# The second layer's second product, in its last two passes, by a seven-product scheme over two quads at a time

## The chip, the cores and the metric

One NeuronCore of a Trainium2 chip runs the whole program. The metric is the device time of one execution in microseconds; less is better. The engines that matter here are PE (TensorE: matrix products, with PEld for its weight loads), DVE (VectorE), ACT (ScalarE), and SP (SyncE), whose queue issues every transfer. POOL (GpSimd) works in the first quarter only.

## The reference

```python
def _moe_ref(x, w_in, w_out):            # first layer, after the attention
    h = x @ w_in
    relu6 = np.clip(h + 3.0, 0.0, 6.0)
    g = h * relu6 / 6.0
    return (g @ w_out).astype(np.float32)

def _moe2_ref(x, w_in, w_out):           # second layer
    h = x @ w_in
    g = np.maximum(0.01 * h, h)
    return (g @ w_out).astype(np.float32)

def reference(...):
    attn_out = _attn_ref(q, k, v)        # 4 x 8 heads, 576 tokens, window 64
    x = attn_out laid out as 2304 tokens x 512
    return _moe2_ref(_moe_ref(x, moe_w_in, moe_w_out), moe2_w_in, moe2_w_out)
```

There are 2304 tokens, the model width is 512 and the hidden width 2048. Inputs and outputs are fp32.

## The kernel before, in words

Every large product is made in pieces of a 128x128 stationary tile and a moving tile of 256 to 512 columns. Each operand is kept as a high half (`h`) and a low half (`l`), both fp32r, and a product is three matmuls: high by high, low by high, high by low. Making the two halves of a tile is a copy (ACT, `copy`, L322) and a subtraction (DVE, `tensor_tensor`, L332).

The first 240 us hold the attention and the first six hidden blocks of the first layer. From there on the hidden width goes in *quads*: 256 hidden columns by 768 tokens by 512 inputs, cut into 2x2x2 blocks. The first product of a quad (x by `w_in`) takes seven block products in place of eight (`SEQ`, the scheme of Strassen in Winograd's form; the matmul is L889, six of 384 columns in each block product, 42 in a quad). The blocks of weights for it are made once (`convert_quad`), written to DRAM (`kept`) and read back in each pass (`fetch`).

The second layer has three passes over the tokens (`NPAIR`, 768 tokens each), and in each pass eight quads. In the first pass the weights of quads 4 to 7 are still being converted; those of quads 0 to 3 were converted ahead, during the first layer. After the seven block products DVE adds partial sums (`plus`, L337), ACT applies the leaky rectifier (L865, L870), and the four blocks C11, C12, C21, C22 are split into halves. The second product (g by `w_out`, `outputs1`, the matmul is L1012) is plain: four blocks by three chunks of 128 tokens by three matmuls, 36 of 512 columns in a quad. It adds up in six PSUM banks over all eight quads, and is copied out once a pass. The outputs of quad i run between the block products of quad i+1, at places that `FILL` names: six units of three matmuls after M6 and six after M7.

The second product of the first layer (`outputs0`, L960) has pieces of 512 and of 256 columns.

The order of the work is written out by `Order`: each step is recorded with what it reads and writes and with an estimated cost; the steps are then placed on the engines, and each engine runs its list in that order. The products of PE are chained, so their order is the one in which they are recorded. On each engine an instruction waits for its inputs and for the buffers it overwrites, and what stands behind it waits too.

## Time and profile before

| | |
|---|---|
| time, median of 3 runs | 849.51 us (847.99 to 850.63) |
| the profiled execution | 850.17 us, of which its span 848.1 us |
| PE busy | 830.9 us, 98% of the span |
| PEld busy | 739.3 us, 87% |
| DVE busy | 540.5 us, 64% |
| ACT busy | 505.9 us, 60% |
| DMA | 201.26 MB, mean 237 GB/s |

The span runs from the first to the last instruction. A row of the timeline gives start, duration, engine, line, operation and the tiles written and read. Matmuls are pipelined: the duration of one is longer than the distance between two starts, so the rate is read from starts. The tiles `h` and `a` and `y` are PSUM banks; `w0h` and `w0l` hold blocks of `w_in`, `w1h` and `w1l` those of `w_out`.

### The profile page before, as it was taken

The page shows a single profiled execution, that of the slowest core. Times are in us where ns is not written, and L with a number is a line of the kernel's source. Part 1 is how long each engine was busy: PE and PEld are TensorE (multiplying, and loading weights), DVE is VectorE, ACT ScalarE, POOL GpSimd, SP SyncE. Part 2 cuts the span into 40 slices and gives each one's busy share as a digit, 9 for nine tenths or more (in the row PEclk, how much of TensorE's full clock was granted, in tenths as well). Part 3 has the DMA queues.
Part 4 walks back from the last instruction along what each step waited for, and adds up shares of the span by engine and source line. Part 5 has one row for each costly group of instructions (what it writes and reads, how often), then busy time and mean ns, then how long its engine had stood idle before and what let it go on. Part 6 is the DMA issues. An engine that isn't in the chain of part 4 may idle for free.

```text
span 848.1 us, 14685 instructions
## 1 busy us (share of the span) xinstructions
PE 830.9 (98%) x5254; PEld 739.3 (87%) x5254; DVE 540.5 (64%) x1184; ACT 505.9 (60%) x1146; POOL 42.5 (5%) x45
## 2 busy tenths in 40 slices
PE   7799999999999999999999999999999999999998
PEld 5578888888999999999999999898998899899986
DVE  5999777878868788878879848888222235222221
ACT  4988878776766665566568457676433344432333
POOL 2222221210000000000000000000000000000000
PEclk9999999999999999999999999999999999999999
DMA  8957485638775879998898747679755564765501
GB/s 272 338 173 262 124 288 200 234 128 281 249 289 186 300 283 319 339 374 270 291 385 304 266 157 251 234 241 366 258 199 166 186 208 158 265 213 163 174 24 75
DMA packets 106329, 201.26 MB, mean 237 GB/s; under 512 B 10768, under 2 KB 22544, under 8 KB 106256
## 3 DMA queue, kind: packets, MB, share of 16 engines
q1 hardware_dynamic: 106256, 200.32, 69.0%
q8 instruction: 42, 0.69, 0.4%
q14 instruction: 31, 0.25, 0.1%
HBM read 153.35 MB, written 46.92 MB: 236 GB/s over the span
## 4 chain that ended last, share of the span: by engine, by line
PE 94%; DVE 2%; DMA 2%; ACT 1%; SPq 0%; issue 0%; DVEq 0%
PE h L889 33%; PE y L1012 16%; PE y L960 9%; PE y L652 9%; PE h L606 9%; PE a L1012 8%; PE a L960 5%; PE a L496 2%; PE h L553 1%; PE a L521 1%; DMA qt<-in_q_dram 1%; DMA st<-in_moe_w_out_dram 1%; PE y L496 1%; DVE ca L360 0%; SPq L340 0%
## 5 line engine op out<-in xcount | busy, mean ns | idle before, releaser
L337 DVE TENSOR_TENSOR qt<-h,qt 128x384 f32<-128x384 f32 x69 | 38.5, 557 | 112.4 <-PE h L889 61.8
L889 PE MATMUL h<-e,w0h 128*128 128x384 f32 x354 | 105.7, 335 | 0.0
L889 PE MATMUL h<-e,w0l 128*128 128x384 f32 x348 | 104.6, 336 | 0.1
L1012 PE MATMUL y<-w1h,at 128*128 128x512 f32 x288 | 97.2, 391 | 0.0
L322 ACT ACTIVATE qt<-h 128x384 f32<-128x384 f32 x77 | 37.6, 488 | 72.0 <-PE h L889 71.8
L960 PE MATMUL y<-at,w1h 128*128 128x512 f32 x240 | 79.4, 391 | 0.0
L889 PE MATMUL h<-xa,w0h 128*128 128x384 f32 x236 | 69.5, 335 | 0.0
L889 PE MATMUL h<-xa,w0l 128*128 128x384 f32 x232 | 68.6, 335 | 0.0
L889 PEld LDWEIGHTS h<-e,w0h 128*128 128x128 f32 x354 | 65.5, 188 | 0.9
L889 PEld LDWEIGHTS h<-e,w0l 128*128 128x128 f32 x348 | 64.4, 188 | 1.3 <-ACT qt L322 0.5
L1012 PEld LDWEIGHTS y<-w1h,at 128*128 128x128 f32 x288 | 54.1, 188 | 10.5
L360 DVE TENSOR_SCALAR ca<-ca 128x512 f32<-128x512 f32 (+1 forms) x128 | 56.3, 447 | 5.5 <-ACT ca L371 4.3
L1012 PE MATMUL y<-w1l,at 128*128 128x512 f32 x144 | 56.6, 393 | 0.0
L960 PEld LDWEIGHTS y<-at,w1h 128*128 128x128 f32 x240 | 45.1, 188 | 8.8
L337 DVE TENSOR_TENSOR r<-h,r 128x384 f32<-128x384 f32 x32 | 17.8, 557 | 53.0 <-ACT r L322 30.2
L1012 PE MATMUL a<-w1h,at 128*128 128x512 f32 x144 | 50.2, 389 | 0.0
L333 POOL TENSOR_TENSOR at<-at,rc 128x512 f32<-128x512 f32 (+1 forms) x36 | 41.1, 1144 | 138.7 <-DVE rc L452 80.3
L960 PE MATMUL a<-at,w1h 128*128 128x256 f32 x240 | 47.8, 282 | 0.0
L960 PE MATMUL y<-at,w1l 128*128 128x512 f32 x120 | 47.2, 394 | 0.0
L371 ACT ACTIVATE ca<-st 128x512 f32<-128x512 f32 x64 | 42.7, 669 | 6.5 <-DMA st<-in_moe_w_out_dram 3.0
L652 PE MATMUL y<-gh,w1h 128*128 128x512 f32 (+1 forms) x120 | 45.8, 382 | 0.0
L332 DVE CUSTOM_DVE_ANT_0 ca<-ca,cr 128x1024 uint16<-128x1024 uint16 x64 | 44.7, 703 | 0.6
(261 smaller groups left out, 2086.0 us busy)
## 6 DMA issues: line engine op xcount, KB each, us to landing
w0h<-kept SPq DMA_DIRECT2D x116, 256.0 KB, 4.1
w0l<-kept SPq DMA_DIRECT2D x115, 256.0 KB, 4.2
w1h<-kept SPq DMA_DIRECT2D x66, 256.0 KB, 4.5
w1l<-kept SPq DMA_DIRECT2D x66, 256.0 KB, 4.8
st<-in_moe_w_in_dram SPq DMA_DIRECT2D x32, 512.0 KB, 5.1
st<-in_moe_w_out_dram SPq DMA_DIRECT2D x32, 512.0 KB, 5.1
kept<-e SPq DMA_DIRECT2D x33, 256.0 KB, 3.7
kept<-gh SPq DMA_DIRECT2D x22, 256.0 KB, 5.4
```

The lines of the kernel that those rows point to most:

```text
L322: a = act(n, lambda: nc.scalar.activation(out=dst(), in_=src(), func=AF.Copy, scale=scale))
L332: d = dve(n, lambda: nc.vector.tensor_tensor(out=dst(), in0=a(), in1=b(), op=alu))
L333: p = pool(n, lambda: nc.gpsimd.tensor_tensor(out=dst(), in0=a(), in1=b(), op=alu))
L337: return [dve(n, lambda: nc.vector.tensor_tensor(out=dst(), in0=a(), in1=b(), op=alu))]
L360: return dve(DM, lambda: nc.vector.tensor_scalar(out=dst(), in0=src(), scalar1=s1, scalar2=s2, op0=op0, **({"op1": op1} if op1 else {})), ...
L371: act(DM, lambda: nc.scalar.activation(out=af(), in_=high().bitcast(F32), func=AF.Abs)),
L496: nc.tensor.matmul(pp()[part * W:(part + 1) * W, c * L:(c + 1) * L], y()[r, i, c, :], x()[r, c, j * W:j * W + L], start=not early, stop=Tr ...
L606: nc.tensor.matmul(ph()[:, 0:n], wt()[:, cs], xt()[:, 0:n], start=(c == 0 and m == 0), stop=(c == NK - 1 and m == 2),)
L652: nc.tensor.matmul(y()[:, 0:n], stat()[:, cs], mov()[:, 0:n], start=(first and m == 0), stop=(last and m == 2))
L889: nc.tensor.matmul(bk()[:, 0:HT], a, b_(), start=(start and j == 0 and q_ == 0), stop=(j == 1 and q_ == 2), skip_group_check=True,)
L960: nc.tensor.matmul(y()[:, d:d + n], a()[:, cs], b_[1]()[:, t0:t0 + n], start=(begins and m == 0), stop=(last and m1 and m == 2), skip_grou ...
L1012: nc.tensor.matmul(y(), a()[:, cs], b_(), start=(first and m == 0), stop=(last and m == 2))
```

## The change

In passes two and three of the second layer the second product also takes seven block products in place of eight, over two quads at a time (`outputs2`). Its blocks are two token halves by two hidden blocks by two halves of the output width, and the two quads of a pair are added up inside PSUM. One block product is three chunks of 128 tokens by two quads by three matmuls, each of 256 columns: 18, and 126 for a pair of quads. Its left operands are A11, A12, A22 and four combinations S1 to S4 (made by DVE in `quad`, and split into halves like the others), its right operands six blocks of `w_out` and of differences of its blocks, made in `convert_quad` (four more tiles for a quad, written to `kept`). They are read back by column halves, in runs of 1 KB (`fetch_y`), into a ring of eight tiles.

PSUM no longer holds the outputs of a pass. Two pairs of banks (`up`, `side`) take the block products in turn, and after each one DVE adds the bank into a sum in SBUF (`add`: one piece of 512 columns and one of 256; in the first pair of a pass some are copies on ACT). There are seven such additions in a pair. The banks `a` now serve the first product of every second quad. `YPLAN` puts the block products of the outputs between those of the first product, one at a time.

Beside that, `xb` (the second layer's input) is three tiles in place of one, so that its parts can be used again as room for the A and S blocks; the ring of `w1` tiles has 6 in place of 7, and the staging ring `st` 4 in place of 3.

```diff
+    WRING = {"w0h": RING, "w0l": RING, "w1h": RING - 1, "w1l": RING - 1}
+    ST = 4
...
-    xb = const.tile([P, NK, NT], F32, name="xb")
...
-    kept = [[dr.tile([11 * P, DM], F32, name=f"kept{j}_{i}") for i in range(n)] for j, n in enumerate(QUADS)]
+    kept = [[dr.tile([(15 if j else 11) * P, DM], F32, name=f"kept{j}_{i}") for i in range(n)] for j, n in enumerate(QUADS)]
...
+    XT = 2 * HT
+    xbt = [buf(f"xb{r}", [P, NK * XT], F32, 1) for r in range(NPAIR)]
...
+    YPLAN = ((0, 1, 0, 1, 1, 0, 1), (0, 1, 0, 1, 1, 0, 0))
...
+            got = [od.slot(("stage", layer), None, None, None, 0, stage_homes(layer)) for _ in range(15 if layer else 11)]
...
+            if layer:
+                got += [od.slot("spare", None, None, None, 0, spare_homes()) for _ in range(4)]
...
+            outs.append((a, af))
+        if layer:
+            (b1, b1f), (b2, b2f) = outs
+
+            def minus(t, tf, h, x, y, reads):
+                op(tensor_tensor(256, lambda: tf()[:, h], x, y, ALU.subtract), reads, [t])
+
+            minus(b1, b1f, L, lambda: b1f()[:, R], lambda: b1f()[:, L], [b1])
+            minus(b1, b1f, R, lambda: b2f()[:, R], lambda: b1f()[:, R], [b1, b2])
+            halves(DM, b1f, [b1], got[11], got[12], got[11], got[12])
+            minus(b2, b2f, R, lambda: b2f()[:, R], lambda: b1f()[:, L], [b1, b2])
+            minus(b2, b2f, L, lambda: b2f()[:, L], lambda: b2f()[:, R], [b2])
+            halves(DM, b2f, [b2], got[13], got[14], got[13], got[14])
+            for j in range(11, 15):
+                keep(j)
...
+    def spare_homes():
+
+        if "spare" not in stage:
+            gone = after_reads(range(1))
+            stage["spare"] = [
+                (None, gone, lambda c=c: xb(c, 0, DM).bitcast(F32R)) for c in range(NK)
+            ]
+        return stage["spare"]
...
+            up, side = bank(tag, 2), bank(tag, 2)
+            twice = "S1" in slots
...
-                    value(r12, *slots["C12"])
+                    if twice:
+                        op(steep(r12), [r12], [r12])
+
+                        def part(t, name):
+                            (kh, h_), (kl, l_) = slots[name]
+                            halves(HT, t, [t], kh, kl, h_, l_)
+
+                        def mix(t, x_, y_, alu):
+                            op(tensor_tensor(HT, t, x_, y_, alu), [x_, y_], [t])
+
+                        mix(r22, r12, r22, ALU.add)
+                        part(r22, "S1")
+                        mix(r12, r11, r12, ALU.subtract)
+                        mix(r11, r22, r11, ALU.subtract)
+                        part(r11, "S2")
+                        part(r12, "S3")
+                        mix(r21, r21, r11, ALU.subtract)
+                        part(r21, "S4")
...
-                            if p < NPAIR - 1:
-                                t = buf("st", [P, DM, 2], U32, bufs=3)
-
-                                def z():
...
-                            else:
-                                t = z = buf(f"xs{c}{'hl'[half]}", [P, DM], F32, 1)
...
+                            k = 3 * half + c
+                            t = sums[k]
+
+                            def z():
+                                return t()[:, 0:DM].bitcast(F32)
+
+                            op(copy(DM, z, y), [y], sum_keys(k))
+                            load_out(P * DM * 4, out[r0:r0 + P, :], z, sum_keys(k))
...
+        YSEQ = (("M1", "A11"), ("M2", "A12"), ("M6", "S2"), ("M5", "S1"), ("M7", "S3"), ("M3", "S4"), ("M4", "A22"))
+        YROWS = {"M1": (7, 0), "M2": (9, 0), "M3": (9, 1), "M5": (11, 0), "M7": (11, 1), "M4": (13, 0), "M6": (13, 1)}
...
+        def settle(early):
+
+            sums.extend(buf(t, [P, DM], F32R, WRING[t]) for t in ("w1h", "w1l") * 3)
+            ywt.extend((None, t, t) for t in [buf(t, [P, DM], F32R, WRING[t]) for t in ("w1h", "w1l") * 3])
+            xbt[0].ops += [*early.prev[1].ops, *(i for t in od.tags[("ring", "spare")] for i in t.ops)]
+            xbt[1].ops += after_reads(range(1, 3)).prev[1].ops
+            free = [buf(f"xb{r}", [P, NK * XT], F32R, 1) for r in range(2)]
...
+            order = units[0:8] + units[16:26] + units[8:16] + old
...
+        def outputs2(p, n, pairs):
+
+            first, last = n == 0, n == QUADS[1] // 2 - 1
+            up = bank("y0"), bank("y1")
+            side = bank("y2"), bank("y3")
+            tiles_ = {}
+
+            def fetch_y(m):
+                hi, half = YROWS[m]
+                for e in range(2):
+                    t = tiles_[m, e] = od.slot("yw", None, None, None, 0, ywt)
+                    src = kept[1][2 * n + e][hi * P:(hi + 2) * P, half * 256:half * 256 + 256].rearrange(
+                        "(m p) n -> p m n", p=P)
+                    load(P * DM * 4, lambda t=t: t().bitcast(F32).rearrange("p (m n) -> p m n", m=2), src, [t],
+                         [("kept", 1, 2 * n + e, hi + j) for j in range(2)])
+
+            def add(b, bk, fresh):
+                i, j = b // 2, b % 2
+                for w, k, o, y in ((DM, b, 0, bk[0]), (256, 4 + i, 256 * j, bk[1])):
+                    t = sums[k]
+                    keys = sum_keys(k) if w == DM else [(t, j)]
+
+                    def dst(t=t, o=o, w=w):
+                        return t()[:, o:o + w].bitcast(F32)
+
+                    def got(y=y, w=w):
+                        return y()[:, 0:w]
+
+                    if fresh:
+                        op(copy(w, dst, got), [y], keys)
+                    else:
+                        op(vector_only(w, dst, got, dst, ALU.add), [y, *keys], keys)
+
+            def send(b):
+                i, j = b // 2, b % 2
...
+            def product(m, x, bk, start):
+                wt = [tiles_[m, e] for e in range(2)]
+                gs_ = [pairs[e][x] for e in range(2)]
+                for chunks in ((0, 1), (2,)):
+                    y = bk[chunks[0] // 2]
+
+                    def fn(chunks=chunks, y=y):
+                        for k, c in enumerate(chunks):
+                            cs = slice(c * P, (c + 1) * P)
+                            for e in range(2):
+                                (_, gh), (_, gl) = gs_[e]
+                                hi, lo = wt[e]()[:, 0:256], wt[e]()[:, 256:512]
+                                for q_, (a, b_) in enumerate(((gh, hi), (gh, lo), (gl, hi))):
+                                    nc.tensor.matmul(
+                                        y()[:, 256 * k:256 * k + 256], a()[:, cs], b_,
+                                        start=(start and k == 0 and e == 0 and q_ == 0),
+                                        stop=(e == 1 and q_ == 2), skip_group_check=True,
+                                    )
+
+                    keys = [kv[0] for e in range(2) for kv in gs_[e]]
+                    op([pe(6 * len(chunks) * (0.0132 + 256 / 2400), fn)], [*wt, *keys], [y], chain=True)
...
+            final = p == NPAIR - 1 and last
+            apart = (bank("h", 2), bank("h", 2)) if final else None
+            order = [YSEQ[k] for k in ((0, 1, 6, 2, 3, 4, 5) if final else range(7))]
...
+                    product(m, x, side if m in ("M2", "M5", "M3") else up, m in ("M1", "M2", "M5"))
+                    if m == "M1":
+                        add(0, up, first)
+                    elif m == "M2":
+                        add(0, side, False)
+                        if last:
+                            send(0)
+                    elif m == "M6":
+                        add(1, up, first)
+                    elif m == "M5":
+                        add(3, side, first)
+                    elif m == "M7":
+                        add(3, up, False)
+                        if last:
+                            send(3)
+                        if final:
+                            add(2, up, False)
+                            send(2)
+                    elif m == "M3":
+                        add(1, side, False)
+                        if last:
+                            send(1)
+                    else:
+                        add(2, up, first)
+                        if last:
+                            send(2)
+
...
+                    if layer and p:
+                        m = (p - 1) * QUADS[1] + i
+                        if m == 0:
+                            settle(early)
+                        wt = ring_tiles(kk)[0:7]
+                        for j, t in enumerate(wt):
+                            load(P * DM * 4, lambda t=t: t().bitcast(F32), kept[1][i][j * P:(j + 1) * P, :], [t],
+                                 [("kept", 1, i, j)])
+                        wt[6].whole = True
+                        slots = places(m)
+                        done_ = m > 1
+                        quad(layer, wt, slots, todo, YPLAN[i % 2] if done_ else (0, 0, 3, 0, 3, 0, 0),
+                             "a" if i % 2 and done_ else "h", flush=i % 2 == 1)
+                        kk += 1
+                        if i % 2:
+                            assert not todo
+                            todo = outputs2(p, i // 2, (both, slots))
```

How the change moves the instructions is shown at two places of the last pass. On PE, before, all of a unit's three matmuls have 512 columns, and the units of a quad's outputs follow each other through the six banks `y0` to `y3`, `a`, `a`:

```order
L889 MATMUL h_8728<-e0_2834,w0h_8579 128x384
L1012 MATMUL y0_8055<-w1h_8492,at_3174 128x512
L1012 MATMUL y0_8055<-w1l_8494,at_3174 128x512
L1012 MATMUL y0_8055<-w1h_8492,at_3174 128x512
L1012 MATMUL y1_8062<-w1h_8492,at_3174 128x512
L1012 MATMUL y1_8062<-w1l_8494,at_3174 128x512
L1012 MATMUL y1_8062<-w1h_8492,at_3174 128x512
```

After it, one block product of the outputs stands between two of the first product, in two banks (`y0` holds two chunks side by side, `y1` the third); `w1h` is the weight tile of the pair's first quad, `w1l` of its second:

```order
L941 MATMUL h_9224<-xa_2856,w0l_8920 128x384
L1209 MATMUL y0_9235<-w1h_7187,xb0_7082 128x256 x3
L1209 MATMUL y0_9235<-w1l_7192,st_7163 128x256 x3
L1209 MATMUL y0_9235<-w1h_7187,xb0_7082 128x256 x3
L1209 MATMUL y0_9235<-w1l_7192,st_7163 128x256 x3
L1209 MATMUL y1_9254<-w1h_7187,xb0_7082 128x256 x3
L1209 MATMUL y1_9254<-w1l_7192,st_7163 128x256 x3
L941 MATMUL h_9210<-e0_2788,w0l_8970 128x384
```

On DVE, before, a quad of the last pass is seven instructions: three additions from the bank `h` (L337) and four subtractions that make low halves (L332).

```order
L337 TENSOR_TENSOR qt_3131<-h_8520,qt_3131 128x384
L332 TENSOR_TENSOR at_3174<-r_3215,at_3174 128x384
L332 TENSOR_TENSOR at_3174<-qt_3131,at_3174 128x384
L337 TENSOR_TENSOR qt_3162<-h_8520,qt_3162 128x384
L332 TENSOR_TENSOR at_3174<-qt_3162,at_3174 128x384
L337 TENSOR_TENSOR qt_3162<-h_8520,qt_3162 128x384
L332 TENSOR_TENSOR at_3174<-r_3204,at_3174 128x384
```

After it, the additions from `y` banks into the sums (`w1h`, `w1l` on the left) stand among those from the first product's bank (`a` here) and the subtractions and combinations of the S blocks:

```order
L346 TENSOR_TENSOR qt_3164<-a_9393,qt_3164 128x384
L341 TENSOR_TENSOR qt_3124<-qt_3124,r_3214 128x384
L346 TENSOR_TENSOR w1l_7143<-y0_9235,w1l_7143 128x512
L346 TENSOR_TENSOR w1l_7159<-y1_9254,w1l_7159 128x256
L341 TENSOR_TENSOR xb0_7082<-qt_3164,xb0_7082 128x384
L341 TENSOR_TENSOR at_3169<-r_3214,at_3169 128x384
L341 TENSOR_TENSOR at_3169<-wx_3217,at_3169 128x384
L341 TENSOR_TENSOR at_3169<-qt_3124,at_3169 128x384
L346 TENSOR_TENSOR w1l_7110<-y2_9283,w1l_7110 128x512
L346 TENSOR_TENSOR w1h_7149<-y3_9299,w1h_7149 128x256
L346 TENSOR_TENSOR r_3206<-a_9393,r_3206 128x384
```

The bank `y2`, `y3` of the second addition is written by the block product that stands, on PE, one block product of the outputs behind that of `y0`, `y1`.

## Rows read from the trace of the kernel before

**Rows 1.** Page: busy time by engine, granted clock, chain by engine.

```profile
PE 830.9 (98%) x5254; PEld 739.3 (87%) x5254; DVE 540.5 (64%) x1184; ACT 505.9 (60%) x1146; POOL 42.5 (5%) x45
...
PEclk9999999999999999999999999999999999999999
...
PE 94%; DVE 2%; DMA 2%; ACT 1%; SPq 0%; issue 0%; DVEq 0%
```

**Rows 2.** Windows: opening, first layer, second layer's first pass, its last two.

```profile
core 0: us, PE busy (x) PEld busy (x) DVE busy (x) ACT busy (x) POOL busy (x), PEclk, DMA share, GB/s
0.00:50.00 50.00, 37.16 (x463) 27.63 (x464) 39.11 (x93) 37.19 (x104) 13.63 (x21) 0.97 0.85 279
400.00:450.00 50.00, 50.00 (x288) 46.77 (x287) 41.55 (x85) 30.32 (x61) 0.00 (x0) 1.00 0.94 342
472.00:596.00 124.00, 124.00 (x629) 112.49 (x628) 93.05 (x178) 75.65 (x149) 0.00 (x0) 1.00 0.71 248
596.00:820.00 224.00, 224.00 (x1123) 202.52 (x1122) 61.21 (x111) 86.97 (x180) 0.00 (x0) 1.00 0.58 190
```

**Rows 3.** Waits of PEld from 232 us on: us in total, times, longest.

```profile
PEld h L889 <- ACT qt L322: 0.5, 1, 0.5
```

**Rows 4.** Timeline of PE, last pass: start, duration; 18 matmuls, then 12.

```profile
823.05 0.39 PE L1012 MATMUL y<-w1h,at 128*128 128x512 f32 x1
...
827.17 0.33 PE L889 MATMUL h<-e,w0h 128*128 128x384 f32 x1
...
829.27 0.39 PE L1012 MATMUL y<-w1h,gh 128*128 128x512 f32 x1
```

**Rows 5.** Timeline of PE, first layer: 12 matmuls of 256 columns.

```profile
302.76 0.28 PE L960 MATMUL a<-at,w1h 128*128 128x256 f32 x1
...
304.19 0.34 PE L889 MATMUL h<-xa,w0l 128*128 128x384 f32 x1
```

**Rows 6.** Chain of waits in order of time: two quads one period apart.

```profile
506.52 5.22 PE h L889 x30
...
522.09 5.22 PE h L889 x30
```

**Rows 7.** Line L960, weight loads at 256 columns: duration min/median/max, ns.

```profile
L960 PEld LDWEIGHTS a<-at,w1h x240: 187/192/192, 247.1 to 477.1; 128*128 128x128 f32 x120
```

**Rows 8.** Groups on DVE and ACT by shape: busy us, mean ns.

```profile
L337 DVE TENSOR_TENSOR qt<-h,qt 128x384 f32<-128x384 f32 x69 | 38.5, 557 | 112.4 <-PE h L889 61.8 <-ACT qt L322 49.8 <-ACT cr L379 0.6
L332 DVE TENSOR_TENSOR st<-ca 128x256 f32<-128x256 f32 x26 | 10.4, 421 | 0.2
L977 DVE TENSOR_TENSOR xb<-y,xb 128x512 f32<-128x512 f32 x12 | 7.7, 684 | 0.0
...
L322 ACT ACTIVATE w0l<-ca 128x512 fp32r<-128x512 f32 x3 | 1.9, 631 | 0.1
```

**Rows 9.** DMA from 0 to 20 us, two of its windows, and a landing time.

```profile
DMA packets 4223, 5.30 MB, mean 265 GB/s; under 512 B 238, under 2 KB 3003, under 8 KB 4222
...
6.00:7.00 1.00, 1.00 (x27) 1.00 (x27) 0.17 (x1) 0.00 (x0) 0.00 (x0) 1.00 1.06 336
7.00:8.00 1.00, 1.00 (x27) 1.00 (x21) 0.42 (x2) 0.44 (x3) 0.00 (x0) 1.00 0.97 334
...
kept<-gh SPq DMA_DIRECT2D x22, 256.0 KB, 5.4
```

**Rows 10.** The end of the span: last matmul, last copy, last transfer.

```profile
843.48 0.39 PE L1012 MATMUL a<-w1h,at 128*128 128x512 f32 x1
...
843.90 0.60 ACT L322 ACTIVATE xs2l<-a 128x512 f32<-128x512 f32 x1
...
844.52 0.33 SPq L1028 DMA_DIRECT2D out_dram<-xs2l  x1
```

**Rows 11.** Longest wait of PE in the opening: us in total, times, longest.

```profile
PE y L483 <- DVE mask_r L1091: 2.5, 1, 2.5
```

More of the change, by code (lines that the diff above doesn't have):

```diff
@@ L715, in convert_quad @@
         if kk is None:
-            got = [od.slot(("stage", layer), None, None, None, 0, stage_homes(layer)) for _ in range(11)]
+            got = [od.slot(("stage", layer), None, None, None, 0, stage_homes(layer)) for _ in range(15 if layer else 11)]
         else:
             got = ring_tiles(kk)
+            if layer:
+                got += [od.slot("spare", None, None, None, 0, spare_homes()) for _ in range(4)]
         got[6].whole = False
@@ L758, in convert_quad, with after_reads @@
             keep(8 + 2 * e)
-        return got
+            outs.append((a, af))
[11 more added lines that the diff above has]
+                keep(j)
+        return got
+    def spare_homes():
[5 more added lines that the diff above has]
+        return stage["spare"]
+    def after_reads(bs):
+        past = od.Buf(None, None, None, None, None)
+        for b in bs:
+            for c in range(NK):
+                past.ops += od.hist[("y1", b, c)][1]
+        gone = od.Buf(None, None, None, None, None)
+        gone.prev = (None, past)
+        return gone
     def paired():
@@ L906, in quad @@
             value = leaky if layer else swish
-            up, side = bank("h", 2), bank("h", 2)
+            up, side = bank(tag, 2), bank(tag, 2)
+            twice = "S1" in slots
             for pos, (m, x) in enumerate(SEQ):
@@ L913, in quad @@
                     plus(r11, side)
-                    value(r11, *slots["C11"])
+                    value(r11, *slots["A11" if twice else "C11"])
                 elif m == "M6":
@@ L919, in quad @@
                     plus(r22, side)
-                    value(r22, *slots["C22"])
+                    value(r22, *slots["A22" if twice else "C22"])
                 elif m == "M4":
-                    if layer:
+                    if twice:
+                        r21 = work()
+                        leaky(r21, *slots["A12"], up)
+                    elif layer:
                         leaky(work(), *slots["C21"], up)
@@ L931, in quad @@
                         fill.pop(0)()
-            while fill:
+            while fill and flush:
                 fill.pop(0)()
@@ L995, in outputs1 @@
             todo, count = [], {}
[L996 to L999 removed]
+            for name, e, half in (("C21", 1, 0), ("C22", 1, 1), ("C11", 0, 0), ("C12", 0, 1)):
                 for c in range(3):
@@ new lines, in go @@
+                            load_out(P * DM * 4, out[r0:r0 + P, :], z, sum_keys(k))
+                    todo.append(go)
+            return todo
+        YSEQ = (("M1", "A11"), ("M2", "A12"), ("M6", "S2"), ("M5", "S1"), ("M7", "S3"), ("M3", "S4"), ("M4", "A22"))
+        YROWS = {"M1": (7, 0), "M2": (9, 0), "M3": (9, 1), "M5": (11, 0), "M7": (11, 1), "M4": (13, 0), "M6": (13, 1)}
+        COME = ("A11", "A22", "A12", "S2", "S1", "S3", "S4")
+        GO = tuple(x for _, x in YSEQ)
+        sums, ywt, halls = [], [], []
@@ L1044, in paired @@
                 inputs(layer, p)
+                if layer and not p:
+                    early = after_reads(range(2))
                 for i in range(QUADS[layer]):
+                    if layer and p:
[15 more added lines that the diff above has]
+                            todo = outputs2(p, i // 2, (both, slots))
+                        both = slots
+                        continue
                     if p == 0 and i >= STAGED[layer]:
```

124 lines of the change are left out of this document (86 added, 38 removed).

## The prediction

> **What bounds the kernel now.** I read the page first. PE is busy for 830.9 of 848.1 us, the chain that ended last is 94% PE, and the granted clock stands at full in every slice; DVE is at 64%, ACT at 60% [rows 1]. Then the windows by stage: PE lacks work only in the opening (37.16 of 50 us); from the first layer's quads on its windows are full [rows 2]. A full window could still hide stalls, since a matmul's row lasts longer than its share of PE, so I looked at the waits: from 232 us to the end the weight-load queue waited once, for 0.5 us [rows 3]. PE is fed without a gap in both layers, and time taken off its work there comes off the span, until something else makes it wait.
>
> The rate per matmul comes from starts. In the last pass 18 matmuls of 512 columns take 823.05 to 827.17, so 0.2289 us each, and the 12 of 384 columns behind them until 829.27, 0.175 each [rows 4]. In the first layer 12 of 256 columns take 302.76 to 304.19, 0.1192 each [rows 5]. A quad of the second layer is 42 x 0.175 + 36 x 0.2289 = 7.35 + 8.24 = 15.59 us; two equal steps of the chain stand 522.09 - 506.52 = 15.57 us apart [rows 6], so the sum is sound.
>
> **The change on PE.** For two quads the outputs cost 72 x 0.2289 = 16.48 us before and 126 x 0.1192 = 15.02 us after: 1.46 us less. Seven products in place of eight would give an eighth, 2.06 us; 0.6 is lost because two half-width matmuls are dearer than one of full width (0.2384 against 0.2289). The two passes hold eight pairs: **-11.7 us**. The first product is as before, so two quads go from 31.14 to 29.7 us.
>
> That rests on a matmul of 256 columns whose weights change every time. The rows for it exist: at 256 columns a weight load lasts 192 ns by its row [rows 7], while the matmuls follow each other every 119 ns [rows 5]; loads lie over each other and over matmuls. Each operand is stationary and moving in the other role there, but the shapes are the same.
>
> The Trainium skill speaks against it (TensorE: Matmul & The Clock Gate, section "The mechanism"): a weight load overlaps matmuls in flight only when it goes to another row group, which loads of the whole array do not. By that rule every matmul would pay its load, and 54 more matmuls in a pair would cost more than the columns save; the trace does not bear it out.
>
> **DVE and ACT in the last two passes.** Before, a quad has 7 instructions on DVE. After, it has 3 additions from the first product's bank, 7 low halves and 4 combinations, 14 of 384 columns at up to 0.557 us, and the pair has seven additions into the sums, 0.684 + 0.421 each [rows 8]. For two quads: 28 x 0.557 + 7 x 1.105 = 15.6 + 7.7 = 23.3 us of 29.7, 79% (before 14 x 0.557 = 7.8 of 31.1). ACT gets three more copies a quad and stays near half. So DVE has room on average; what matters is how long a bank may wait. In the order, the outputs' block products alternate between two pairs of banks. Between two uses of one pair stand one output product (18 x 0.119 = 2.15 us) and three or four of the first product (1.05 us each), at the end of a pair of quads four of the first product alone: 4.2 to 6.3 us, in which DVE has to do 1.1 us. Behind a late addition on DVE stands the next one from the first product's bank, and PE waits for both. Of the first product's banks, M4 must find M7's copied, with 2.15 us between, where ACT needs 0.5; before, 4.1 us stood there. I take no loss in the steady part. If the cover fails, an addition that is late by one instruction costs 0.56 us, and by a whole addition 1.1 us.
>
> **Conversions.** A quad's conversion gains four combinations of 256 columns and two splits of 512: on DVE 4 x 0.421 and two subtractions, for which I take the 0.684 of the addition of that width, so 3.05 us; on ACT 2 x 0.631 = 1.26 us [rows 8]; and four stores of 256 KB. Four conversions lie in the first layer, four in the second layer's first pass. There DVE is at 93.05 of 124 us, 75% [rows 2], and 12.2 us more make it 85%; at 400 us it is 83% already while PE is full. So they hide, at a cost between 0 and, if all of DVE's extra work came onto the path, 24 us; I take the end near the rows, **+0.5**. The four staging places of the conversions made ahead are reused after a store, which lands in 5.4 us [rows 9], and 15 tiles go through them in place of 11; ACT can be held there, and behind it the copies for PE.
>
> **The step from the first pass to the second.** The last quad's four extra tiles lie in `xb`'s first part, where the new A11 goes: on ACT its copy has to wait until their stores have landed, some 5 us by [rows 9], and the next copies out of PSUM stand behind it. By my count of products the copy has 3 to 4 us to spare before the next bank is needed: 0 to 2 us once, I take **+0.5**.
>
> **Transfers.** In the last two passes a quad reads 14 tiles of 256 KB in place of 11, 3.67 MB in 14.85 us: 247 GB/s where the windows now show 190 at a share of 0.58 [rows 2]. At 400 us the core moves 342 GB/s at 0.94 with PE full. Half of the tiles come in runs of 1 KB in place of 2 KB. No row shows such runs alone; the nearest are those of the opening, where 3003 of 4223 packets are under 2 KB (the keys' runs are 768 bytes) and the rate is 334 to 336 GB/s at a share of about 1 [rows 9]. By that the new load is at 247/335 = 74%: no cost. The other end is below, as a rival.
>
> **The ends.** The end now is the last matmul, a copy of 0.60 us, and a transfer of 256 KB [rows 10]. After, seven block products run alone (15.0 us, DVE needs half of it), then come an addition of 0.42 us and a transfer of half the size: **-0.3**, between -0.6 and +0.7 (an addition of 512 columns queued ahead). In the opening the fourth staging buffer lets two weight loads go out earlier and turns some DVE work around; PE waits 12.8 us there, at most 2.5 at a time [rows 2, 11]. Nothing in the trace says which way this goes: 0, between -2.5 and +2.5.
>
> **Sum.** 850.17 - 11.7 + 0.5 + 0.5 - 0.3 = 839.2 us, against the profiled execution's 850.17 (span 848.1 and 2.1 around it). The median of the runs is 0.66 lower, at 849.51, so the forecast is **838.5 us**.
>
> **Rivals.**
> - DVE gives part of it back. It is an in-order list, and an addition may stand behind a subtraction whose high half ACT has not made; then the next block product waits. For it: 79% load with two kinds of deadlines, where it had 25%. Against: 4 to 6 us of slack. Priced at one late addition (1.1 us) in each of eight pairs: +8.8, **847 us**; at half of that 843.
> - The transfers become the bound, the case on the slower side. If a run of 1 KB costs as much as one of 2 KB, it decides: now 11 x 128 runs take 0.58 x 15.57 = 9.0 us of the engines, 6.4 ns each; after, 7 x 128 + 7 x 256 = 2688 runs take 17.2 us a quad, more than PE's 14.85. Over sixteen quads: 16 x (17.2 - 15.57) = +26, **876 us**. The point from which it decides is a run of 1 KB at 5.1 ns, 79% of the larger one's; the rows of the opening say about 3.1 (1024 bytes at 335 GB/s).
> - The conversions jam DVE and ACT in the first pass: half of the 24 us on the path gives -11.7 + 12, **850 us**. Against it stands the full PE at 83% of DVE.
> - The weight loads set the pace. If each load's 0.192 us stood alone, 126 would take 24.2 us against 16.48: +62, over **910 us**. The spacing of 119 ns excludes it as far as a trace can.
>
> **Chances.** The forecast in its own range (836 to 842): 0.62. DVE gives part back (842 to 847): 0.20, and with all of it gone (847 to 852): 0.05. The conversions jam: 0.04, mostly near no change or slower. The transfers: 0.04. The weight loads: under 0.01. A faster opening or shorter waits than I know of (below 836): 0.05. A measurement of this kernel can tell about 0.3% from no change, 2.5 us. Faster 0.87, same 0.06, slower 0.07. The range of 8 in 10: 834.8 to 846.5 us; the likeliest case's own is 836 to 842.
>
> **What would show it.** In the profile of the changed kernel: matmuls of 256 columns in the last two passes at 0.119 us from start to start; two quads of these passes 29.7 us apart on the chain; windows there with PE full, DVE near 70 to 80%, DMA at a share of 0.7 to 0.8 and near 245 GB/s; no wait of PE on DVE but a few tenths. I am wrong if the chain shows DVE or DMA in these passes, if PE has idle time between 470 and 620 us, or if the first 240 us end more than 2.5 us earlier or later than now.

## The result, and the profile after it

The changed kernel takes **839.58 us** (median of four runs, 839.06 to 840.0) against 848.97 for the kernel before on the same chip (847.99 to 850.63); the ratio is 0.9891, 95% interval 0.9876 to 0.9907. The forecast was 838.5 us, with a range of 834.8 to 846.5. Its profiled execution took 839.61 us, with a span of 837.8, 10.3 less than the 848.1 of the profile of before. Two executions, one of the kernel before with 1342.71 us and one of all_but_strassen with 4668.34, lie far from all others and are left out of every median here.

The page of the changed kernel, busy time and chain (what ended last, followed back to the start), to be read against [rows 1]:

```profile
PE 819.0 (98%) x5686; PEld 750.8 (90%) x5686; DVE 665.5 (79%) x1442; ACT 539.0 (64%) x1218; POOL 41.9 (5%) x45
...
PE 92%; DVE 3%; DMA 3%; issue 0%; ACT 0%; SPq 0%
```

432 more matmuls are done in 11.9 us less busy time. Three windows, with the columns of [rows 2] (length, busy time of PE, PEld, DVE, ACT and POOL, granted clock, DMA share, GB/s): the opening, the second layer's first pass, its last two:

```profile
0.00:50.00 50.00, 35.73 (x414) 26.26 (x414) 35.31 (x87) 34.47 (x100) 11.20 (x19) 0.93 0.85 279
472.00:596.00 124.00, 123.57 (x627) 111.91 (x626) 102.79 (x205) 81.50 (x160) 0.00 (x0) 1.00 0.75 265
596.00:820.00 224.00, 224.00 (x1562) 222.82 (x1561) 161.50 (x314) 121.17 (x249) 0.00 (x0) 1.00 0.80 256
```

In the last two passes PE is as full as before, though DVE now works 161.5 of 224 us (72%) and the weight loads fill their queue. The first pass has lost 0.43 us of PE, the opening 1.4, at a lower granted clock. The waits of both PE queues from 232 us to the end [rows 3] have one event:

```profile
PEld h L941 <- ACT qt L331: 0.8, 1, 0.8
PE h L941 <- ACT qt L331: 0.4, 1, 0.4
```

So no block product waits for a bank, a tile or an addition. The chain has a period of two quads. Here are an equal step of the kernel before, 16 quads behind the one at 506.52 [rows 6], then the first block product of three pairs in the changed kernel, and the durations of line L1209's weight loads (minimum, median, maximum, as in [rows 7]):

```profile
755.69 5.22 PE h L889 x30
```

```profile
614.04 2.13 PE y L1209 x18
...
643.62 2.15 PE y L1209 x18
...
791.61 2.13 PE y L1209 x18
```

```profile
L1209 PEld LDWEIGHTS y<-w1l,xb x162: 187/188/193, 618.3 to 829.4; 128*128 128x128 f32 x162
```

(791.61 - 614.04) / 6 = 29.595 us for a pair, where two quads took (755.69 - 506.52) / 8 = 31.147. A block product of 18 matmuls lasts 2.14 us, 0.119 for each, with loads of 0.188 us by row under them.

**Where the time is lost again.** On PE, in the opening:

```profile
28.69 0.66 PE L530 MATMUL h<-ident_r,at 128*128 128x128 f32 x4
34.31 1.12 PE L562 MATMUL a<-at,xb 128*64 128x64 f32 x16 [4.96 <-DMA xb<-in_v_dram]
```

SP's queue shows why; first before, then after (start, duration, DMA):

```profile
22.81 0.33 SPq L340 DMA_DIRECT2D st<-in_moe_w_in_dram  x1
25.54 0.33 SPq L340 DMA_DIRECT2D xb<-in_v_dram  x1
26.43 0.33 SPq L340 DMA_DIRECT2D at<-in_v_dram  x1
28.25 0.33 SPq L340 DMA_DIRECT2D st<-in_moe_w_out_dram  x1
```

```profile
21.78 0.33 SPq L349 DMA_DIRECT2D st<-in_moe_w_in_dram  x1
22.80 0.33 SPq L349 DMA_DIRECT2D st<-in_moe_w_out_dram  x1
24.86 0.33 SPq L349 DMA_DIRECT2D st<-in_moe_w_in_dram  x1
25.29 0.38 SPq L349 DMA_DIRECT2D xb<-in_v_dram  x1
```

Three weight loads of 512 KB, not one, now go out ahead of the fifth item's `v` loads, on DMA engines whose share is about 1. And the granted clock, the third number from the end of a window's row, falls after the idle 5 us.

```profile
30.00:32.00 2.00, 0.00 (x0) 0.00 (x0) 1.83 (x5) 2.00 (x5) 0.00 (x0) 1.00 1.02 327
34.00:36.00 2.00, 1.69 (x32) 1.72 (x32) 0.62 (x1) 0.45 (x1) 0.00 (x0) 0.50 0.87 327
38.00:40.00 2.00, 1.82 (x4) 1.01 (x5) 1.97 (x5) 2.00 (x10) 0.00 (x0) 0.50 0.90 347
42.00:44.00 2.00, 2.00 (x24) 1.43 (x26) 0.80 (x3) 0.60 (x1) 0.00 (x1) 1.00 0.00 0
```

From 34 to 40 us PE ran at 0.50 (1.2 of 2.4 GHz). What the wait and the clock cost together is read from what follows.

A fixed place to read what the opening costs is the chain's step of 18 matmuls at 257.25 us, early in the first layer's quads; behind it PE is never idle for long:

```profile
257.25 3.12 PE h L889 x18
```

```profile
259.40 3.12 PE h L941 x18
```

From this step to the end of the span it is 848.1 - 257.25 = 590.85 us before and 837.8 - 259.40 = 578.4 after. So the last two passes and what lies around them gave 12.45 us, and the opening took 2.15 back. All kernels that follow are compared by these two numbers, each from one profiled execution.

### The profile page after: what moved, and what is told of

It is laid out like the page before. It is cut to its first block, busy times and chain, and to the rows that moved or that the text cites. A ratio compares the mean times of both kernels' runs of the same rounds, so it can differ in the third digit from the quotient of the medians.

```text
span 837.8 us, 16098 instructions
## 1 busy us (share of the span) xinstructions
PE 819.0 (98%) x5686; PEld 750.8 (90%) x5686; DVE 665.5 (79%) x1442; ACT 539.0 (64%) x1218; POOL 41.9 (5%) x45
## 4 chain that ended last, share of the span: by engine, by line
PE 92%; DVE 3%; DMA 3%; issue 0%; ACT 0%; SPq 0%
PE h L941 28%; PE y L1209 14%; PE y L1035 10%; PE h L615 8%; PE y L661 8%; PE a L941 6%; PE y L1084 5%; PE a L1035 5%; PE a L1084 3%; PE a L505 1%; PE h L562 1%; PE a L530 1%; DMA xb<-in_v_dram 1%; DMA at<-in_v_dram 1%; DMA qt<-in_q_dram 1%; PE a L562 1%
## 5 line engine op out<-in xcount | busy, mean ns | idle before, releaser
L941 PE MATMUL h<-e,w0l 128*128 128x384 f32 x306 | 90.3, 335 | 0.0
L941 PE MATMUL h<-e,w0h 128*128 128x384 f32 x270 | 82.0, 335 | 0.4 <-ACT qt L331 0.4
L941 PE MATMUL h<-xa,w0l 128*128 128x384 f32 x204 | 59.3, 335 | 0.0
L941 PE MATMUL h<-xa,w0h 128*128 128x384 f32 x180 | 54.1, 335 | 0.0
L941 PEld LDWEIGHTS h<-e,w0h 128*128 128x128 f32 x270 | 50.0, 188 | 1.1 <-ACT qt L331 0.8
L388 ACT ACTIVATE cr<-st 128x512 uint32<-128x512 uint32 x64 | 42.4, 669 | 7.6 <-DMA st<-in_moe_w_out_dram 3.7
L385 DVE SCALAR_TENSOR_TENSOR ca<-st,ca 128x512 uint32<-128x512 uint32 x64 | 46.5, 737 | 0.6
L661 PE MATMUL y<-gl,w1h 128*128 128x512 f32 (+1 forms) x120 | 44.4, 370 | 0.0
L661 PE MATMUL y<-gh,w1l 128*128 128x512 f32 (+1 forms) x120 | 44.3, 369 | 0.0
L331 ACT ACTIVATE at<-qt 128x384 fp32r<-128x384 f32 x69 | 35.9, 521 | 8.3 <-DVE qt L904 5.3
```

The source lines that it names most:

```text
L331: a = act(n, lambda: nc.scalar.activation(out=dst(), in_=src(), func=AF.Copy, scale=scale))
L385: op([dve(DM, lambda: nc.vector.scalar_tensor_tensor(out=a(), in0=high(), scalar=0xC0000000, in1=a(), op0=ALU.bitwise_and, op1=ALU.bitwise ...
L388: op([act(DM, lambda: nc.scalar.activation(out=r(), in_=st()[:, :, 0], func=AF.Copy, scale=2.0 ** -29))], [st], [r])
L661: nc.tensor.matmul(y()[:, 0:n], stat()[:, cs], mov()[:, 0:n], start=(first and m == 0), stop=(last and m == 2))
L941: nc.tensor.matmul(bk()[:, 0:HT], a, b_(), start=(start and j == 0 and q_ == 0), stop=(j == 1 and q_ == 2), skip_group_check=True,)
```

## The experiments

Step and rest of every profiled execution, and the median of the runs. The kernel before ran again beside three groups of them, with medians of 848.20 (22 runs; four_st_alone, hold_weights, last_pass_only, all_but_strassen), 848.23 (17 runs; three_st_plan, no_combinations, additions_twice, output_weights_2k) and 848.06 (9 runs; after_again, three_st_six). The ratio is to the runs of the same group, for the changed kernel to the 848.97 us above.

| kernel | median us | ratio to before, 95% | step at | step to end |
|---|---|---|---|---|
| before (profiled: 850.17) | 848.97 | | 257.25 | 590.85 |
| before_again (one run) | 846.99 | | 254.25 | 590.65 |
| changed | 839.58 | 0.9876 to 0.9907 | 259.40 | 578.4 |
| after_again | 839.98 | 0.9885 to 0.9915 | 258.12 | 578.9 |
| four_st_alone | 848.22 | 0.9993 to 1.0014 | 257.25 | 590.25 |
| hold_weights | 837.80 | 0.9862 to 0.9900 | 256.10 | 578.5 |
| three_st_plan | 837.72 | 0.9849 to 0.9886 | 254.49 | 579.5 |
| three_st_six | 837.18 | 0.9857 to 0.9887 | 255.82 | 579.7 |
| last_pass_only | 846.92 | 0.9972 to 0.9994 | 258.28 | 586.2 |
| all_but_strassen | 852.39 | 1.0036 to 1.0074 | 258.16 | 592.1 |
| no_combinations | 839.65 | 0.9876 to 0.9909 | 260.03 | 579.2 |
| additions_twice | 850.44 | 1.0007 to 1.0031 | 259.17 | 589.5 |
| output_weights_2k | 840.27 | 0.9885 to 0.9920 | 258.11 | 578.5 |

**four_st_alone**, on the kernel before.

```diff
+    WRING = {"w0h": RING, "w0l": RING, "w1h": RING - 1, "w1l": RING - 1}
+    ST = 4
...
-        st = buf("st", [P, DM, 2], U32, bufs=3)
+        st = buf("st", [P, DM, 2], U32, bufs=ST)
...
```

> The kernel before with the fourth staging buffer st and the shorter w1 rings, nothing else. Theory (the fourth buffer lets weight loads go out ahead of attention's v loads, PE waits for these, and that is the 1.8 us by which the first layer's quads start later in the changed kernel): the chain's step of 18 matmuls that stands at 234.49 us in the kernel before and at 236.31 in the changed one stands between 235.3 and 236.3 here (only one weight load has moved ahead of the pair of v loads, not two), and the time is 0.8 to 1.8 us above before. Rival (the later start comes from the split of the first layer's additions or from the rest of the new order): 234.5 us, and no change of the time within 0.5 us.

The step that stood at 234.49 stands at 234.87, the later one at 257.25 as before, and the time is unchanged. The buffer and the shorter rings alone cost nothing; my theory is refuted in this form. One weight load did move ahead of a pair of `v` loads here, where the whole change moves two. What remained was that larger change of order.

**hold_weights**, on the changed kernel.

```diff
-    HOLD = {(0, 0): (2,), (1, 0): (6,)}
+    HOLD = {(0, 0): (2,), (1, 0): (6,), (1, 1): (8,)}
```

> The changed kernel with one entry more in the table HOLD: the second feature block's w_out load goes out behind the v loads of the fifth attention item. Theory: the 5.0 us wait of PE for xb<-in_v_dram in the opening falls below 1 us, the granted clock stays at 1.00 from 28 to 46 us, the first layer's quads start within 0.5 us of 234.5 as in the kernel before, and the time is 1.3 to 2.0 us below the changed kernel's: about 837.9 us. Rival (something else in the opening, DVE or ACT, is late as well and takes the place of the wait): quads at 236 us or later, 839.6 us.

In the profiled execution the wait for `xb` is gone, the clock is 1.00 from 28 to 46 us, the rest is the same 578.5, and the step stands at 256.10. That is 1.15 us ahead of its place in the first profile of the kernel before, more than the 0.5 that I allowed. PE still waits elsewhere there, at most 2.5 us at a time. So this wait comes from the order of these loads. The time by itself does not show it: the profiled execution was the fastest of four (836.34 us, the others 837.50 to 839.62), and the changed kernel's nine lie between 837.80 and 841.24.

**last_pass_only** and **all_but_strassen**, on the changed kernel (with FROM = 2 and 3; 3 is none of the passes). The lines left out give the plain outputs of the last pass their own tiles and order back.

```diff
...
-                    if layer and p:
-                        m = (p - 1) * QUADS[1] + i
+                    if layer and p >= FROM:
+                        m = (p - FROM) * QUADS[1] + i
```

> The changed kernel with Strassen's scheme for the outputs in the last pass alone; the middle pass has the plain outputs as before. Theory (the gain is 1.55 us for each pair of quads on PE, measured from start to start in the changed kernel, and nothing else): four pairs give -6.2, the opening gives +1.7, the step with its wait +0.4, the tail +0.2: 3.9 us below before, 845.5 us; two quads 31.15 us apart in the middle pass, 29.6 in the last. Rival (a part of the gain or of the loss comes once, with the change of passes): more than 1.5 us off that.

> The changed kernel with the plain outputs in all three passes: fourth staging buffer, extra combinations of the output weights, their stores and the spare places stay, and nobody reads the extra tiles. Theory (opening +1.7, one wait of 0.4 in the conversions of the first pass, conversions otherwise hidden): 1.5 to 2.5 us above before, 851.5 us. Rival (the conversions or their stores cost more than the waits show, hidden in the gain): more than 3 us above before.

Against the profile of before, last_pass_only's is 846.26 - 850.17 = -3.9 us, as expected; but that profile was itself 2.0 us above the median of the later runs, and by medians it is only -1.3. By medians all_but_strassen is 4.2 us slower than before, beyond what the rival named (more than 3). The step shows where: both stand at 258.2, like the changed kernel's, and behind it all of the change but Strassen's scheme adds only 1.3 us to 590.85. So most of the 4.2 lies in the opening, below, and not in the conversions. Where one wait of 0.4 us was expected, both kernels have two, at 575 us, in the conversion of the first pass's last quad but one:

```profile
PE h L942 <- ACT w0h L332: 1.0, 1, 1.0
PE h L942 <- DVE w0l L342: 0.3, 1, 0.3
```

The changed kernel has 0.43 us there. From the step to the end of the last matmul it is 588.4 us with the scheme in no pass, 582.0 with it in the last, and 574.7 with it in both. The last pass gives 6.4 us, and so does the middle one once the 0.9 us by which the changed kernel waits less at 575 are taken off; four pairs at 1.55 are 6.2. Pairs 29.6 us apart stand in the last pass of last_pass_only and quads 15.57 apart in its middle one. So the gain is PE's, per pair. What PE waits for in the conversions differs from order to order: 0.4 us in one, 1.3 in another.

**no_combinations**

```diff
...
-            minus(b1, b1f, L, lambda: b1f()[:, R], lambda: b1f()[:, L], [b1])
...
-            halves(DM, b2f, [b2], got[13], got[14], got[13], got[14])
-            for j in range(11, 15):
-                keep(j)
+            for j in range(11, 15):
+                op([("SP", 0.62, lambda j=j: nc.sync.dma_start(
+                    out=kept[1][i][j * P:(j + 1) * P, :], in_=got[j - 4]().bitcast(F32)))], [got[j - 4]], [("kept", 1, i, j)])
...
```

The lines left out also take away the four added staging tiles and the places in `xb`'s first part: a quad's conversion uses 11 tiles again, and the four extra stores read plain ones.

> The changed kernel without the four combinations and two splits that a quad's conversion gained; the four extra rows are still stored and read, but hold the plain output weights (this part of the computation is left out). Theory (the conversions are hidden but for the one wait of 0.4 us at 575): from the step of 18 matmuls near 259 to the end 577.9 to 578.4 us, DVE in the first pass of the second layer near 93 of 124 us in place of 102.8, the wait at 575 gone. Rival (they hold PE up in ways the waits do not show): more than 2 us less, 576 or below.

```profile
472.00:596.00 124.00, 123.26 (x625) 111.61 (x624) 91.52 (x175) 75.99 (x149) 0.00 (x0) 1.00 0.75 263
```

DVE is 11.3 us less busy in the first pass, and PE gains nothing. The wait at 575 is gone, as expected, but another stands at 483, 0.74 us for another copy of ACT (`r`). So the rest is 579.2, 0.8 above the upper end of what I gave, and the time is the same (839.65 us against 839.58). What holds is that the added instructions are hidden; a small wait is there without them too.

**additions_twice**

```diff
                         op(vector_only(w, dst, got, dst, ALU.add), [y, *keys], keys)
+                        op(vector_only(w, dst, got, dst, ALU.add), [y, *keys], keys)
```

> The changed kernel with every addition of a partial output into the sums done twice (the outputs then hold each partial product twice). It adds 7 x (0.60 + 0.34) = 6.6 us to DVE for each pair of quads of 29.6 us, by the distances of such additions in the changed kernel's tail: DVE goes from 0.73 to 0.95, and a pair of output banks is held some 2 us in place of 1. Theory (a bank has 4 us or more before it is needed again, and DVE has room): PE stays full in most of the two passes, less than 3 us slower than the changed kernel. Rival (DVE's list is tight already and a late addition reaches PE): PE waits for DVE in every pair, 1 us or more each, 8 us or more in all.

It loses 11 us against the changed kernel. The theory's 3 us are far exceeded, and the rival's total (8 us or more) came about, but not in its way, a wait in every pair. Two windows, then the chain here, and one step of the changed kernel's:

```profile
650.00:700.00 50.00, 50.00 (x360) 50.00 (x359) 44.34 (x89) 25.31 (x49) 0.00 (x0) 1.00 0.78 247
700.00:750.00 50.00, 47.38 (x327) 46.09 (x327) 47.22 (x97) 26.49 (x55) 0.00 (x0) 1.00 0.82 260
```

```profile
614.99 2.13 PE y L1210 x18
...
644.57 2.15 PE y L1210 x18
...
674.20 2.14 PE y L1210 x18
...
715.48 0.47 DVE xs1l L341
715.95 0.47 DVE xs2l L341
716.42 0.47 DVE xs3l L341
...
719.07 2.40 PE y L1210 x18
...
723.56 2.13 PE y L1210 x18
```

```profile
718.72 2.13 PE y L1209 x18
```

With DVE at 89% the pairs are still 29.6 us apart: no loss at all. About 1.2 us had been lost before, between the step at 259 and the first pair (614.99 against 614.04), where no addition is doubled. At the change of passes DVE also makes the next pass's input halves (`xs1l` and others); the chain goes over to DVE from 704 to 719, and PE loses 3.9 us (the block product at 718.72 in the changed kernel stands at 723.56 here, the one at 696.53 at 697.49). Then nothing more until the end, where the last additions stand alone and cost 6.4 (845.73 against 834.53 for the last one's end, less 4.84).

**output_weights_2k**

```diff
-                    src = kept[1][2 * n + e][hi * P:(hi + 2) * P, half * 256:half * 256 + 256].rearrange(
-                        "(m p) n -> p m n", p=P)
+                    src = kept[1][2 * n + e][(hi + half) * P:(hi + half + 1) * P, :]
```

> The changed kernel with the second layer's output weights stored so that a block of high and low parts is one run of 2 KB for each partition where it was two of 1 KB; in exchange the stores, and the first pass's reads of these weights, have runs of 1 KB. Theory (a run costs by its bytes: 3.4 ns for 1 KB in the changed kernel by its share of 0.80, 6.4 ns for 2 KB by the share of 0.58 before): the DMA share from 596 to 820 us is 0.76 to 0.80, PE is as full, and the time is within 1 us of the changed kernel, apart from what the new order does to the opening. Rival (runs, not bytes, are paid): the share falls below 0.65 there and rises in the first pass.

```profile
596.00:820.00 224.00, 224.00 (x1567) 223.03 (x1566) 162.33 (x315) 120.94 (x249) 0.00 (x0) 1.00 0.78 255
```

0.78 at 255 GB/s, and the same 578.5 us; the changed kernel had 0.80 at 256 in its first profile and 0.78 at 256 in after_again. The share does not fall below 0.65, so here a run of 1 KB or 2 KB was paid by its bytes and not by its number.

**before_again, after_again, three_st_plan, three_st_six.** The first two are the two kernels unchanged; the others are the changed kernel with this, and three_st_six with 6 in place of 2 * PLAIN:

```diff
         st = buf("st", [P, DM, 2], U32, bufs=ST)
+        seq = od.tags[id(sb), "st"]
+        if 3 < len(seq) <= 2 * PLAIN:
+            st.prev = (seq[-2], seq[-4])
```

> The kernel before, profiled once more. Its runs spread over 846 to 851 us, and the execution that the prediction rests on took 850.2. Theory (the opening differs from execution to execution, the rest doesn't): from the step of 18 matmuls at 257.25 to the end it is 590.9 us again (within 0.3), and the step stands earlier, at 254.5 to 256.5. Rival (the spread lies in the two layers): the step at 257.2 and the rest 588 to 590 us.

> The changed kernel, profiled and timed once more beside the one with an altered opening. Theory: from the step of 18 matmuls to the end 578.4 us (within 0.3), the step at 258.5 to 260, PE waiting 3.5 to 5.5 us for xb<-in_v_dram; 839.6 us. Rival: the wait was of one execution alone, the step stands below 257.5.

> The changed kernel with its four staging buffers, but the planner is told of three while it orders the loads of the first layer's plain feature blocks; on SP the weight loads and v loads of the opening then stand as in the kernel before. Theory (what the changed kernel loses in the opening is the order of these loads): the wait of PE for xb<-in_v_dram is below 1 us, the chain's step of 18 matmuls that stands at 257.25 before and 259.40 in the changed kernel stands between 255.5 and 257.5, from it to the end of the span it is 578.4 us as in the changed kernel, and the time is 1.5 to 3 us below the changed kernel's 839.6. Rival (other parts of the opening's order, on DVE and ACT, cost it): the step at 258.5 or later, 839 us or more.

> As three_st_plan, but the planner is told of three staging buffers for the first six loads alone, which leaves the second layer's order as in the changed kernel. Theory: step of 18 matmuls at 254.5 to 257.5, from it to the end 578.4 (the wait of 1.4 us in the conversions of three_st_plan is 0.4 again), 836.5 to 837.7 us, the fastest of all. Rival: the opening falls out otherwise with this order, 839 us or more.

The kernel before starts its quads 3.0 us earlier in the second profile than in the first, with the same rest. In after_again the wait for `xb` is there again (3.8 us); its step, 258.12, and its rest, 578.9, lie a little outside what I gave, and so does before_again's step. The two kernels with the order of before's loads have the step at 254.5 and 255.8, the changed kernel at 258.1 to 259.4. On SP's queue of three_st_six one weight load stands ahead of these `v` loads again:

```profile
21.31 0.33 SPq L349 DMA_DIRECT2D st<-in_moe_w_in_dram  x1
23.55 0.33 SPq L349 DMA_DIRECT2D xb<-in_v_dram  x1
24.97 0.33 SPq L349 DMA_DIRECT2D at<-in_v_dram  x1
25.35 0.43 SPq L349 DMA_DIRECT2D st<-in_moe_w_out_dram  x1
```

three_st_six is the fastest of all kernels, 837.18 us (836.74 to 837.83) against 839.98 (837.80 to 841.24) for the changed one beside it. The 578.4 that I expected for both was missed: in the first pass of three_st_six PE waits another 0.9 us for a copy of ACT, and in that of three_st_plan 1.4 for DVE (`w0l`).

The same order of loads (three weight loads, then four `v` loads) stands in all seven profiles whose step is at 258.1 or later, and in none of the other six. The longest wait at the matmuls that need these `v` loads is for `xb` in six of the seven (2.1 to 5.0 us); in all_but_strassen the profile puts 3.9 us down to ACT (`cr`), a step in converting such a weight load.

## Why the prediction was right

**PE's gain: right, but 6% too small.** Forecast -11.7, measured 8 x (31.147 - 29.595) = -12.4. The mechanism is the one forecast; the term was mis-sized by the spacings, read from single stretches. Over the pairs a 256-column matmul takes 2.14 / 18 = 0.1189 us, not 0.1192, and 512 columns 0.2294, not 0.2289 (a pair less its 84 x 0.1742, over 72): 0.07 us a pair.

**The weight loads: as the rows said.** Loads of the whole array, 188 ns each, run at a spacing of 119 ns. Had each load stood alone, 1008 matmuls at 0.07 us more would have cost some 70 us, an estimate from these rows. The prediction weighed one rule of the Trainium skill against this (TensorE: Matmul & The Clock Gate, section "The mechanism": a load overlaps matmuls only in another row group), and the measurement decides against that rule here. The same section also names a second case, a load that goes to the background weight buffer; the spacing fits that one, though no run here shows where a load went.

**DVE and ACT in the last two passes: right.** No wait. DVE's share was 72%, not 79%: the row of an addition of 384 columns lasts 0.557 us, but a following one starts after 0.47, so adding up rows overstates the load. additions_twice shows no loss in the steady part at 89%.

**Transfers: right.** 0.80 and 256 GB/s for the forecast's 0.74 and 247 (730 to 800 us, between the passes' changes: 0.78 and 251). With 6.4 ns for a 2 KB run, 0.80 x 14.8 us less 896 of these leaves 6.1 us for 1792 runs: 3.4 ns for 1 KB, where 3.1 was taken and 5.1 would have decided.

**Conversions: right, +0.4 for +0.5**, but taking the added work out gains nothing: that wait goes and another comes (no_combinations), so what the 0.43 us are due to is open. By the letter of the prediction this idle time of PE between 470 and 620 us was a sign of being wrong; it is too small to change the account. DVE reached 83% in the first pass, 85% was forecast.

**The step from the first pass to the second: the mechanism was wrong.** No wait stands at the change; the only one is at 575, inside the first pass, and the term above already counts it. ACT there:

```profile
573.71 0.62 ACT L331 ACTIVATE w0h<-st 128x512 fp32r<-128x512 f32 x1
574.23 0.51 ACT L331 ACTIVATE at<-r 128x384 fp32r<-128x384 f32 x1
574.64 0.47 ACT L331 ACTIVATE qt<-h 128x384 f32<-128x384 f32 x1
```

A conversion's copy and a split stand ahead of the copy out of PSUM (`qt<-h`) that PE waits for. The +0.5 should have been 0.

**The end: -0.5 for -0.3.** From the last matmul to the end it is 3.7 us, before 4.2 [rows 10]. The last matmuls, the last product's two additions and the last, smaller transfer:

```profile
833.40 0.69 DVE L346 TENSOR_TENSOR w1l<-y,w1l 128x512 f32<-128x512 f32 x1 [0.20 <-PE y L1209]
...
833.56 0.52 PE L1209 MATMUL y<-st,cr 128*128 128x256 f32 x3
834.11 0.42 DVE L346 TENSOR_TENSOR w1h<-y,w1h 128x256 f32<-128x256 f32 x1
834.60 0.45 SPq L1116 DMA_DIRECT2D out_dram<-w1h  x1
```

**The opening: the step that failed.** "Nothing in the trace says which way this goes: 0, between -2.5 and +2.5." The sentence before it names what turned out to matter, two weight loads that go out earlier. They go ahead of loads that PE waits for, on DMA engines whose share is about 1 there [rows 9]; they are 1 MB, or by estimate some 3 us at 335 GB/s, and [rows 11] shows attention as a chain with little cover. Profile against profile it cost 2.15 us; over the seven profiles with the changed order (the step at 258.1 to 260.0, mean 258.8) and the six without (254.3 to 257.3, mean 255.9) it is 2.9.

The prediction also read the clock as full in every slice of the page [rows 1]. A slice is 21 us long; the same trace of the kernel before, cut finer, has a nearly idle stretch and the lower clock behind it:

```profile
44.00:46.00 2.00, 0.51 (x5) 0.24 (x3) 2.00 (x4) 1.91 (x11) 1.02 (x1) 1.00 0.37 78
48.00:50.00 2.00, 2.00 (x31) 1.67 (x24) 1.85 (x6) 1.92 (x5) 0.90 (x1) 0.50 0.74 186
```

All nine profiles with the step at 257 or later have such a stretch in the opening; the four with an earlier step (before_again, hold_weights, three_st_plan, three_st_six) have none. Over the 48 later executions of the kernel before, those with a mean granted clock of 0.999 or 1.000 have spans of 844.0 to 846.4 us, those with 0.993 have 846.8 to 848.2. So the clock goes with the time of the opening; how much of it the clock costs by itself, and why one program falls into such a stretch in some executions only, was not settled.

That the forecast of 838.5 came so near is in part luck. For the span the terms are -12.4 + 0.4 + 0 - 0.5 + 2.15 = -10.35, where -10.3 was measured between the two profiles and -11.0 forecast: a gain that was too small and an opening put at nothing partly cancel. And the forecast started too high: its median of three was 849.51, the 48 later runs of the kernel before have 848.16. Against these the changed kernel's nine (median 839.61) are 8.6 us faster, not 11.0. The gain behind the step is 12.1 us by the two profiles of each kernel, which leaves some 3.5 us for the opening, by estimate, more than the 2.5 that the prediction allowed it.

## What to carry to other kernels

Where PE is full and never waits, count its starts: here the work taken off came off that stretch to within 6% of the count. A second engine could go to 89% there without loss, as long as what it owed had some microseconds to spare. Look for the loss where the cover is thin, at the opening, at changes of pass and at the end. And when a change gives a planner one more buffer, read the new order of the loads in the opening: a transfer that may go earlier can go ahead of one that is waited for. Look at the granted clock there in windows of a few microseconds, not in the slices of the page.

## What the runs showed of the hardware

- After 5.0 us without a matmul PE ran at a granted clock of 0.50 for some 6 us (changed kernel, 34 to 40 us); a stretch with the lower clock stands in every profile with a late opening and in none with an early one.
- DVE additions out of PSUM that follow each other start 0.60 us (512 columns), 0.47 (384) and 0.34 (256) apart, where their rows last 0.684, 0.557 and 0.421.
- The first 255 us of the kernel before varied by 3.0 us between two executions, the 590 behind them by 0.2.
- Weight loads of 188 ns by their rows, with new weights for each matmul, ran under matmuls of 256 columns that follow each other every 119 ns.
- In the last two passes a run of 1 KB took 3.4 ns over the 16 DMA engines and one of 2 KB 6.4 ns, by the shares of 0.80 and 0.58.
